# Another order of the instructions in the attention period, and another border to the FFN

## The chip, the cores and the metric

The kernel runs on one core of one Trainium2 chip. The metric is the device time of one execution in microseconds. TensorE (PE; its weight loads are PEld) multiplies and transposes, VectorE (DVE), ScalarE (ACT) and GpSimd (POOL) work on elements, SyncE (SP) issues the DMAs. Each engine works through its instructions in program order and waits on semaphores for the others.

## The reference

Attention with pooled queries, and a feed-forward network on its output.

```python
B, H, S, D = 4, 8, 1152, 64
q_pool = q.reshape(B, H, S // 2, 2, D).mean(axis=3)          # 576 queries per head
scores = 1 / sqrt(D) * q_pool @ k.T                          # 576 x 1152
scores = scores - scores.max(axis=-1)
attn = exp(scores); attn = attn / (attn.sum(axis=-1) + 1e-9)
x = (attn @ v) -> transposed to 2304 x 512
h = x @ w_in                                                 # 512 -> 2048
out = (h * tanh(softplus(h))) @ w_out                        # 2048 -> 512, float32
```

## The kernel before

**Attention.** The work is cut into 32 steps: batch (4), pair of heads (4), half of the queries (2). The two heads of a pair lie side by side in the partitions. A step has 9 chunks of 128 keys and 288 queries per head, and each chunk is one call of these functions:

- QK (L200): scores of a chunk, one matmul per head on 64 rows of the array each (shape 64*128), into a PSUM tile of the pool psS, which has two buffers; a chunk overwrites the tile of the chunk two before it.
- CP (L215) copies the scores to T3 in SBUF on ACT; MX (L218) keeps the running maximum over the chunks on DVE. Both read the PSUM tile.
- MT (L228), TMAX (L235), MB (L240): the maximum over the 128 keys of a chunk. Five transposes, one reduction on DVE, six transposes that spread the maximum over the partitions again (tile Mb in PSUM).
- SUB (L251, DVE) and EXP (L256, ACT): subtract and exponentiate, in four groups of 2, 2, 2 and 3 chunks (GR).
- PV (L270): values of a chunk, one matmul per head on 64 columns of the array each (shape 128*64), nine chunks added up in the PSUM tile pv, one buffer; PVE (L283, ACT) takes it out.
- ADD (L260, POOL) adds up the exponentials; FIN0 (L290) sums them over the partitions on TensorE, again in shape 128*64.
- FLN, FEX (ACT, logarithm and exponential), FU (POOL), FE, FX (DVE) multiply by the reciprocal of the sums and write xT. For the last step LX (L315) does it on DVE alone, with a reciprocal instruction.

Once per pair of steps QP (L122, POOL) pools the queries and TG (L139) transposes keys and queries, TGc (L153, ACT) takes them out. load_q, load_k and load_v issue the DMAs on SP.

**FFN.** x and the weights are split into a high and a low part (split_x, conv), H_ (L488) makes 12 matmuls of a hidden block, A_g, A_gh, D_gl the activation, O_ (L521) six matmuls of the output. 144 such blocks run after the attention; the first ones lie between the last values.

**What sets the order.** Every call is an entry of the list `plan` (L598 on) with a time in units of a step; the list is sorted by that time and called in that order. The times do nothing else: on the chip an engine takes its instructions in this order and as early as their semaphores allow. STEP (L337) has one time per call, added to the number of the step; PAIR (L397) the same per pair of steps. So parts of three steps overlap. XE (L569) places the first splits of x, TH and TA (L572) the first FFN blocks, LAST, LATE and GONE (L573 to L575) the end of the last two steps.

Of the kernel before, what the change touches and what calls it, by code (L numbers as in the profile page):

```python
# [12 lines left out]
ALU = mybir.AluOpType  # L13
# [4 lines left out]
def f32(ap):  # L18
    return ap.bitcast(F32)
# [3 lines left out]
def tile_pooled_attention_then_mish_ffn(ctx: ExitStack, tc: tile.TileContext, q, k, v, moe_w_in, moe_w_out, out):  # L23
# [5 lines left out]
    P = 128  # L29
# [37 lines left out]
    if True:  # L67
# [125 lines left out]
        rmaxs, Mbs, pvs, accs = {}, {}, {}, {}  # L193
# [46 lines left out]
        def MB(i):  # L240
            m = Ts.pop(i)
            Mb = ps1.tile([P, 2, 512], F32, tag="Mb", name=f"Mb{i}")
            for n, k0, k1, j, a in (
                (0, 0, P, 0, 0), (1, 0, P, 0, 128), (3, 0, P, 1, 64), (4, 0, P, 1, 160), (2, 0, 64, 0, 224), (2, 64, P, 1, 0)
            ):
                pe.transpose(  # L246
                    Mb[:, j, a:a + k1 - k0], m[k0:k1, n:n + 1].to_broadcast([k1 - k0, P]), ident[k0:k1, k0:k1]
                )
            Mbs[i] = Mb
# [20 lines left out]
        def PV(i, c):  # L270
            vn = vs[i // 2]
            if c == 0:
                pvs[i] = ps1.tile([P, 512], F32, tag="pv", name=f"pv{i}")
            for j in range(2):
# [4 lines left out]
                    start=(c == 0),  # L279
                    stop=(c == NC - 1),  # L280
# [48 lines left out]
        def FX(i):  # L329
# [8 lines left out]
            (QK, 0, -0.564),  # L338
            (CP, 0, -0.504),
            (QK, 1, -0.428),  # L340
            (MX, 1, -0.396),
            (CP, 1, -0.363),
            (QK, 2, -0.351),
            (MX, 2, -0.314),
            (QK, 3, -0.298),
            (CP, 2, -0.293),
            (MX, 3, -0.195),
            (QK, 4, -0.183),
            (CP, 3, -0.164),
            (CP, 4, -0.151),  # L350
            (MX, 4, -0.150),
            (QK, 5, -0.137),
            (CP, 5, -0.003),
            (QK, 6, 0.031),
            (MX, 5, 0.064),
            (CP, 6, 0.102),
            (QK, 7, 0.170),
            (MX, 6, 0.245),
            (CP, 7, 0.280),
            (MX, 7, 0.464),  # L360
            (QK, 8, 0.527),
            (CP, 8, 0.530),
            (MX, 8, 0.540),
            (MT, 0.653),
            (TMAX, 0.719),
            (MB, 0.814),
            (SUB, 1, 0.826),
            (SUB, 0, 0.867),
            (EXP, 1, 0.990),
            (SUB, 2, 1.091),  # L370
            (EXP, 0, 1.173),
            (PV, 0, 1.204),
            (PV, 1, 1.215),
            (ADD, 0, 1.267),
            (EXP, 2, 1.369),
            (SUB, 3, 1.494),
            (PV, 2, 1.536),
            (ADD, 1, 1.570),
            (PV, 3, 1.572),
            (EXP, 3, 1.607),  # L380
            (ADD, 2, 1.635),
            (PV, 4, 1.654),
            (PV, 5, 1.857),
            (PV, 6, 1.868),
            (ADD, 3, 1.906),
            (ADD, 4, 1.907),
            (PV, 7, 2.090),
            (FIN0, 2.105),
            (PV, 8, 2.130),
            (PVE, 2.178),  # L390
            (FLN, 2.247),
            (FEX, 2.397),
            (FU, 2.451),
            (FE, 2.604),
            (FX, 2.705),
        ]
        PAIR = [  # L397
            (QP, -2.081),
            (TG, 1, -1.246),
            (TGc, 1, -1.241),  # L400
            (TG, 2, -1.181),
            (TGc, 2, -1.088),
            (TG, 0, -1.039),
            (TGc, 0, -0.962),
            (TG, 3, -0.265),
            (TGc, 3, -0.240),
# [3 lines left out]
        ]  # L410

# [61 lines left out]
        def split_x(u, c):  # L473
# [5 lines left out]
            (dve if u > 2 and c in XD else pool).tensor_tensor(xl[:, c], src, f32(xh[:, c]), ALU.subtract)  # L479

# [84 lines left out]
        LW = -0.5  # L565
# [99 lines left out]
```

## Time and profile before

| | |
|---|---|
| runs, median (lowest to highest) | 896.43 us (896.0 to 898.17) |
| profiled execution: span from its first to its last instruction (the profile gives no other time of it) | 892.8 us |
| TensorE busy | 870.2 us, 97% of the span |
| VectorE busy | 596.7 us, 67% |
| ACT busy | 541.5 us, 61% |
| POOL busy | 455.8 us, 51% |
| mean granted TensorE clock | 0.993 |

The shares are means over two very different parts: in the attention, up to about 470 us, all four engines are busy; after it the FFN keeps TensorE busy alone. A TensorE instruction's end is modelled, its start is measured. "Idle before" is the time in which an engine had nothing to do before an instruction, with what ended it.

### The profile page before, as it was taken

How to read it: one execution, taken by the hardware profiler on the slowest of the kernel's cores; microseconds unless marked ns; L12 is line 12 of the kernel's file. 1: busy time of each engine (PE TensorE's matmuls, PEld its weight loads, DVE VectorE, ACT ScalarE, POOL GpSimd, SP SyncE). 2: the span in 40 equal slices, each digit the busy share in tenths (PEclk: the TensorE clock that was granted, in tenths of full speed). 3: DMA queues.
4: the chain of work that ended last, by engine and by line, in shares of the span. 5: the costliest groups of instructions: out<-in, count | busy, mean ns of one | idle time of the engine just before them, and what ended most of it. 6: DMA issues, size and time to landing. Idle time of an engine off the chain costs nothing. (4 is left out here: it accounts for less than half of the span.)

```text
span 892.8 us, 14677 instructions
## 1 busy us (share of the span) xinstructions
PE 870.2 (97%) x5668; PEld 589.5 (66%) x5668; DVE 596.7 (67%) x812; ACT 541.5 (61%) x999; POOL 455.8 (51%) x268
## 2 busy tenths in 40 slices
PE   6899999999999999999998999999999999999997
PEld 4444444444444444444446889999999999999996
DVE  4889988998889888998897753444455334432222
ACT  4788888888888888888888563333333233322221
POOL 1489888988889888998888530111111011100000
PEclk9899999999999999999999999999999999999999
DMA  6422323132321323131200120111112011001112
GB/s 177 130 49 59 80 54 80 27 81 54 80 59 49 80 54 80 28 80 54 75 2 1 48 94 9 57 48 32 55 65 71 24 48 48 24 1 48 48 48 70
DMA packets 75109, 50.74 MB, mean 57 GB/s; under 512 B 37408, under 2 KB 68640, under 8 KB 75040
## 3 DMA queue, kind: packets, MB, share of 16 engines
q1 hardware_dynamic: 75040, 49.82, 20.1%
q8 instruction: 44, 0.72, 0.3%
q14 instruction: 25, 0.20, 0.1%
HBM read 45.09 MB, written 4.72 MB: 56 GB/s over the span
## 5 line engine op out<-in xcount | busy, mean ns | idle before, releaser
L206 PE MATMUL s<-qT,kT 64*128 64x288 f32 x1152 | 210.7, 453 | 11.2 <-DVE rmax L223 7.2
L512 DVE TENSOR_TENSOR gl<-g,gh 128x256 fp32r<-128x256 f32 x144 | 68.8, 479 | 227.1 <-ACT gh L507 201.1
L502 ACT ACTIVATE g<-h 128x256 f32<-128x256 f32 x144 | 55.7, 387 | 242.5 <-PE h L497 242.5
L216 ACT COPY T<-s 128x576 f32<-128x576 f32 x288 | 181.2, 641 | 33.7 <-DVE rmax L223 15.2
L254 DVE TENSOR_TENSOR T<-T,Mb 128x1152 f32<-128x1152 f32 (+1 forms) x128 | 191.4, 1496 | 11.1 <-PE Mb L246 11.0
L275 PE MATMUL pv<-T,vn 128*64 128x288 f32 x1152 | 192.7, 425 | 1.9 <-ACT pvs L286 1.4
L223 DVE TENSOR_TENSOR rmax<-s,rmax 128x576 f32<-128x576 f32 x224 | 169.0, 754 | 34.2 <-ACT T L216 28.3
L460 POOL TENSOR_TENSOR wl<-wt,wh 128x512 fp32r<-128x512 f32 x32 | 41.8, 1308 | 251.8 <-ACT wh L457 207.9
L266 POOL TENSOR_TENSOR acc<-acc,T 128x1152 f32<-128x1152 f32 x64 | 168.9, 2638 | 2.7 <-ACT T L258 0.2
L258 ACT ACTIVATE T<-T 128x1152 f32<-128x1152 f32 (+1 forms) x128 | 165.9, 1296 | 6.8 <-DVE T L254 4.8
L206 PEld LDWEIGHTS s<-qT,kT 64*128 64x128 f32 x1152 | 89.3, 189 | 115.1 <-issue 40.4
L497 PE MATMUL h<-xh,wh 128*128 128x256 f32 x576 | 162.0, 281 | 0.0
L497 PE MATMUL h<-xh,wl 128*128 128x256 f32 x576 | 161.8, 281 | 0.0
L497 PE MATMUL h<-xl,wh 128*128 128x256 f32 x576 | 161.6, 281 | 0.0
L275 PEld LDWEIGHTS pv<-T,vn 128*64 128x64 f32 x1152 | 63.3, 135 | 88.4 <-issue 57.9
L497 PEld LDWEIGHTS h<-xh,wh 128*128 128x128 f32 x576 | 108.7, 189 | 8.1 <-issue 2.2
L497 PEld LDWEIGHTS h<-xl,wh 128*128 128x128 f32 x576 | 108.9, 189 | 6.0
L264 POOL TENSOR_TENSOR acc<-T 128x1152 f32<-128x1152 f32 x32 | 84.7, 2646 | 49.5 <-ACT T L258 46.0
L497 PEld LDWEIGHTS h<-xh,wl 128*128 128x128 f32 x576 | 109.2, 190 | 0.0
L530 PE MATMUL o<-wh,gh 128*128 128x512 f32 x146 | 57.8, 396 | 1.0 <-ACT xT L542 1.0
L530 PE MATMUL o<-wl,gh 128*128 128x512 f32 x146 | 57.5, 394 | 0.0
L530 PE MATMUL o<-wh,gl 128*128 128x512 f32 x146 | 57.3, 392 | 0.0
(381 smaller groups left out, 1101.2 us busy)
## 6 DMA issues: line engine op xcount, KB each, us to landing
qn<-in_q_dram SPq DMA_DIRECT2D x32, 288.0 KB, 3.8
vn<-in_v_dram SPq DMA_DIRECT2D x16, 576.0 KB, 4.9
kn<-in_k_dram SPq DMA_DIRECT2D x30, 288.0 KB, 4.1
ri<-in_moe_w_in_dram SPq DMA_DIRECT2D x64, 128.0 KB, 2.2
ro<-in_moe_w_out_dram SPq DMA_DIRECT2D x16, 512.0 KB, 3.5
out_dram<-xT SPq DMA_DIRECT2D x18, 256.0 KB, 2.6
T<-in_k_dram SPq DMA_DIRECT2D x2, 288.0 KB, 4.5
```

Source lines behind the costliest of these rows:

```text
L206: pe.matmul(s[:, j, 0:HQ], kT[64 * j:64 * j + 64, c], qT[64 * j:64 * j + 64, hf * HQ:(hf + 1) * HQ], start=True, stop=True,)
L216: act.copy(T3[:, i % 2, c], ss[i, c])
L223: dve.tensor_tensor(r, ss[i, c], T3[:, i % 2, 0] if c == 1 else r, ALU.max)
L254: dve.tensor_tensor(x, x, Mbs[i][:, :, 0:HQ].unsqueeze(1).to_broadcast([P, w, 2, HQ]), ALU.subtract)
L258: act.activation(x, x, AF.Exp, scale=0.0625)
L264: pool.tensor_tensor(accs[i], t[:, 0:2], t[:, 2:4], ALU.add)
L266: pool.tensor_tensor(accs[i], accs[i], t[:, 2 * n + 2:2 * n + 4], ALU.add)
L275: pe.matmul(pvs[i][64 * j:64 * j + 64, 0:HQ], vn[:, j, c, :], T3[:, i % 2, c, j], start=(c == 0), stop=(c == NC - 1),)
L497: pe.matmul(h[:, 0:UT], a, b, start=(m == 0), stop=(m == len(seq) - 1))
L502: act.activation(g, hs[bu, f], AF.Mish)
L512: dve.tensor_tensor(gl, ch.pop((bu, f)), f32(gs[bu, f][0]), ALU.subtract)
L530: pe.matmul(os_[bu][t], x, y, start=(first and m == 0), stop=(last and m == 2))
```

## The change

STEP gets two times per call, the first for even steps, the second for odd ones, so the two steps of a pair may have different orders. The times of STEP, PAIR and XE are new: score chunks mostly come in twos (6 and 7, 8 and the next step's 0, 1 and 2), value chunks in runs of two to four, and no longer from 0 to 8, so PV counts its calls to know the first and the last. MB gives its two 64-row transposes to a call of its own, MBb. split_x of the first three blocks becomes split_h (ACT) and split_l (POOL), 1.892 steps later. At the border the last two steps (BYREC) both end by FIN0 and LX; END gives times of their own to calls of steps 30 and 31; the first FFN blocks (TH, TA) and the reuse of memory (T_REST) move.

```diff
@@ -190,7 +190,7 @@
             load_q(1)
             load_k(1)
 
-        rmaxs, Mbs, pvs, accs = {}, {}, {}, {}
+        rmaxs, Mbs, pvs, pvn, accs = {}, {}, {}, {}, {}
 
@@ -240,12 +240,14 @@
         def MB(i):
             m = Ts.pop(i)
             Mb = ps1.tile([P, 2, 512], F32, tag="Mb", name=f"Mb{i}")
-            for n, k0, k1, j, a in (
-                (0, 0, P, 0, 0), (1, 0, P, 0, 128), (3, 0, P, 1, 64), (4, 0, P, 1, 160), (2, 0, 64, 0, 224), (2, 64, P, 1, 0)
-            ):
-                pe.transpose(
-                    Mb[:, j, a:a + k1 - k0], m[k0:k1, n:n + 1].to_broadcast([k1 - k0, P]), ident[k0:k1, k0:k1]
-                )
+            Mbs[i] = Mb, m
+            for n, j, a in ((0, 0, 0), (1, 0, 128), (3, 1, 64), (4, 1, 160)):
+                pe.transpose(Mb[:, j, a:a + P], m[:, n:n + 1].to_broadcast([P, P]), ident)
+
+        def MBb(i):
+            Mb, m = Mbs[i]
+            for k, j, a in ((0, 0, 224), (64, 1, 0)):
+                pe.transpose(Mb[:, j, a:a + 64], m[k:k + 64, 2:3].to_broadcast([64, P]), ident[k:k + 64, k:k + 64])
             Mbs[i] = Mb
 
         def SUB(i, g):
@@ -269,15 +271,16 @@
 
         def PV(i, c):
             vn = vs[i // 2]
-            if c == 0:
+            pvn[i] = pvn.get(i, 0) + 1
+            if pvn[i] == 1:
                 pvs[i] = ps1.tile([P, 512], F32, tag="pv", name=f"pv{i}")
             for j in range(2):
                 pe.matmul(
                     pvs[i][64 * j:64 * j + 64, 0:HQ],
                     vn[:, j, c, :],
                     T3[:, i % 2, c, j],
-                    start=(c == 0),
-                    stop=(c == NC - 1),
+                    start=(pvn[i] == 1),
+                    stop=(pvn[i] == NC),
                 )
 
@@ -335,79 +338,81 @@
 
         LQ, LK = -3.4, -2.2
         STEP = [
-            (QK, 0, -0.564),
-            (CP, 0, -0.504),
-            (QK, 1, -0.428),
-            (MX, 1, -0.396),
-            (CP, 1, -0.363),
-            (QK, 2, -0.351),
-            (MX, 2, -0.314),
-            (QK, 3, -0.298),
-            (CP, 2, -0.293),
-            (MX, 3, -0.195),
-            (QK, 4, -0.183),
-            (CP, 3, -0.164),
-            (CP, 4, -0.151),
-            (MX, 4, -0.150),
-            (QK, 5, -0.137),
-            (CP, 5, -0.003),
-            (QK, 6, 0.031),
-            (MX, 5, 0.064),
-            (CP, 6, 0.102),
-            (QK, 7, 0.170),
-            (MX, 6, 0.245),
-            (CP, 7, 0.280),
-            (MX, 7, 0.464),
-            (QK, 8, 0.527),
-            (CP, 8, 0.530),
-            (MX, 8, 0.540),
-            (MT, 0.653),
-            (TMAX, 0.719),
-            (MB, 0.814),
-            (SUB, 1, 0.826),
-            (SUB, 0, 0.867),
-            (EXP, 1, 0.990),
-            (SUB, 2, 1.091),
-            (EXP, 0, 1.173),
-            (PV, 0, 1.204),
-            (PV, 1, 1.215),
-            (ADD, 0, 1.267),
-            (EXP, 2, 1.369),
-            (SUB, 3, 1.494),
-            (PV, 2, 1.536),
-            (ADD, 1, 1.570),
-            (PV, 3, 1.572),
-            (EXP, 3, 1.607),
-            (ADD, 2, 1.635),
-            (PV, 4, 1.654),
-            (PV, 5, 1.857),
-            (PV, 6, 1.868),
-            (ADD, 3, 1.906),
-            (ADD, 4, 1.907),
-            (PV, 7, 2.090),
-            (FIN0, 2.105),
-            (PV, 8, 2.130),
-            (PVE, 2.178),
-            (FLN, 2.247),
-            (FEX, 2.397),
-            (FU, 2.451),
-            (FE, 2.604),
-            (FX, 2.705),
+            (QK, 0, -0.5640, -0.5584),
+            (CP, 0, -0.4042, -0.4268),
+            (QK, 1, -0.3837, -0.4118),
+            (QK, 2, -0.3395, -0.3676),
+            (MX, 1, -0.3197, -0.2976),
+            (MX, 2, -0.2628, -0.2408),
+            (CP, 1, -0.2498, -0.3491),
+            (CP, 2, -0.2033, -0.1585),
+            (QK, 3, -0.1849, -0.2352),
+            (QK, 4, -0.1407, -0.1056),
+            (MX, 3, -0.1181, -0.1833),
+            (MX, 4, -0.0612, -0.0387),
+            (CP, 3, -0.0587, -0.1195),
+            (QK, 5, 0.0172, -0.0614),
+            (CP, 4, 0.0823, 0.0864),
+            (MX, 5, 0.0835, 0.1060),
+            (CP, 5, 0.1429, 0.1655),
+            (QK, 6, 0.1527, 0.1835),
+            (QK, 7, 0.1969, 0.2277),
+            (MX, 6, 0.2282, 0.2507),
+            (MX, 7, 0.2850, 0.3076),
+            (CP, 6, 0.2876, 0.3102),
+            (CP, 7, 0.3445, 0.3722),
+            (QK, 8, 0.3974, 0.3918),
+            (MX, 8, 0.4747, 0.4973),
+            (CP, 8, 0.5342, 0.5567),
+            (MT, 0.5357, 0.5638),
+            (TMAX, 0.5963, 0.6255),
+            (MB, 0.6761, 0.7042),
+            (MBb, 0.7532, 0.7486),
+            (SUB, 0, 0.8666, 0.7871),
+            (EXP, 0, 0.9701, 0.9804),
+            (SUB, 1, 1.0113, 0.9887),
+            (SUB, 2, 1.1559, 1.1334),
+            (EXP, 1, 1.2264, 1.2039),
+            (PV, 0, 1.3117, 1.2407),
+            (ADD, 0, 1.3313, 1.3504),
+            (PV, 2, 1.3481, 1.4854),
+            (SUB, 3, 1.3575, 1.3349),
+            (EXP, 2, 1.4746, 1.4124),
+            (PV, 1, 1.4797, 1.3173),
+            (PV, 3, 1.5200, 1.3537),
+            (ADD, 1, 1.5913, 1.6104),
+            (EXP, 3, 1.6349, 1.6900),
+            (PV, 5, 1.7675, 2.1034),
+            (ADD, 2, 1.7928, 1.8231),
+            (PV, 8, 1.9331, 2.1397),
+            (PV, 4, 1.9734, 1.8085),
+            (ADD, 3, 1.9942, 2.0245),
+            (PV, 7, 2.0687, 2.0670),
+            (ADD, 4, 2.1024, 2.1328),
+            (PV, 6, 2.1090, 2.0267),
+            (PVE, 2.1820, 2.2046),
+            (FIN0, 2.2809, 2.2714),
+            (FLN, 2.3836, 2.4113),
+            (FEX, 2.4924, 2.4490),
+            (FE, 2.5303, 2.5472),
+            (FU, 2.5518, 2.5327),
+            (FX, 2.6512, 2.5981),
         ]
         PAIR = [
-            (QP, -2.081),
-            (TG, 1, -1.246),
-            (TGc, 1, -1.241),
-            (TG, 2, -1.181),
-            (TGc, 2, -1.088),
-            (TG, 0, -1.039),
-            (TGc, 0, -0.962),
-            (TG, 3, -0.265),
-            (TGc, 3, -0.240),
+            (QP, -1.7894),
+            (TG, 1, -1.2869),
+            (TGc, 1, -1.1948),
+            (TG, 2, -1.1438),
+            (TGc, 2, -1.0804),
+            (TG, 0, -1.0176),
+            (TGc, 0, -0.9498),
+            (TG, 3, -0.0969),
+            (TGc, 3, 0.0605),
             (load_q, LQ),
             (load_k, LK),
             (load_v, 0.2),
         ]
+
 
         pieces = [(f, io) for io in range(2) for f in range(BLK[0])]
         pieces += [(f, io) for f in range(BLK[0], NF) for io in range(2)]
@@ -478,6 +483,13 @@
             act.copy(xh[:, c], src)
             (dve if u > 2 and c in XD else pool).tensor_tensor(xl[:, c], src, f32(xh[:, c]), ALU.subtract)
 
+        def split_h(u, c):
+            act.copy(x_tiles(u)[0][:, c], xT[:, c, u * UT:(u + 1) * UT])
+
+        def split_l(u, c):
+            xh, xl = x_tiles(u)
+            pool.tensor_tensor(xl[:, c], xT[:, c, u * UT:(u + 1) * UT], f32(xh[:, c]), ALU.subtract)
+
         def acc(n):
             u, t = divmod(n, UT // P)
             w = DM // UT
@@ -562,17 +574,35 @@
 
         CV2 = [0, 0, 0, 1, 2, 3]
         CV3 = [0, 1, 2, 3, 4, 5]
-        LW = -0.5
+        LW, REUSE = -0.5, -0.438
         XD, ED = (2, 3), ()
         CVD = [4, 6, 6, 8, 9, 10]
         SPL = [0, 0, 1, 1]
-        XE = [10.955 + 2 * n for n in range(9)] + [28.955, 29.955, 30.6]
+        XE = [5.349, 7.349, 9.349, 11.349, 13.349, 15.349, 17.349, 19.349, 21.349, 23.349, 25.349, 27.349]
+        XL = 1.892
         XT = (-0.20, -0.19, -0.18, -0.17)
-        T3F, DT, XS, T_REST = 1.14, 0.2, 0.5, 1.76
-        TH, TA = (-0.30, -0.05, 0.60), 0.62
-        LAST = {FIN0: 1.70, LX: 1.75}
-        LATE = {FIN0: 0.60, FLN: 0.62, FEX: 0.63, FU: 0.65, FE: 0.66, FX: 0.70}
-        GONE = (FIN0, FLN, FEX, FE, FU, FX)
+        T3F, DT, XS, T_REST = 1.14, 0.2, 0.5, 1.92
+        TH, TA = (-0.31, 0.22, 0.47), 0.52
+        BYREC = (NS - 2, NS - 1,)
+        GONE = [(i, fn) for i in BYREC for fn in (FLN, FEX, FE, FU, FX)]
+        END = {
+            (PV, NS - 1, 0): 0.25,
+            (PV, NS - 1, 1): 0.26,
+            (PV, NS - 1, 2): 0.33,
+            (PV, NS - 1, 3): 0.34,
+            (PV, NS - 1, 4): 0.5,
+            (PV, NS - 1, 5): 0.51,
+            (PV, NS - 1, 6): 0.7,
+            (PV, NS - 1, 7): 0.71,
+            (PV, NS - 1, 8): 0.72,
+            (EXP, NS - 1, 3): 0.45,
+            (PVE, NS - 2): 0.21,
+            (EXP, NS - 1, 1): 0.2,
+            (FIN0, NS - 2): 0.6,
+            (LX, NS - 2): 0.62,
+            (FIN0, NS - 1): 1.87,
+            (LX, NS - 1): 1.9,
+        }
         FLOW = [
             (H_, 0), (convs, 0), (A_g, 0), (A_gh, 0), (D_gl, 0), (split,), (O_, 3), (EV, 3, 0), (convs, 1),
             (convs, 5), (convs, 4), (convs, 3), (convs, 2), (EV, 3, 1),
@@ -596,11 +626,14 @@
             open_pool("x3", 1)
 
         plan = []
-        for fn, *a, t in STEP:
-            plan += [(i + t, fn, i, *a) for i in range(NS - 1 if fn not in LATE else NS - 2)]
-            plan += [(NS - 1 + t, fn, NS - 1, *a)] if fn not in GONE else []
-        plan += [(NS + t, fn, NS - 1) for fn, t in LAST.items()]
-        plan += [(NS + t, fn, NS - 2) for fn, t in LATE.items()]
+        for fn, *a, t0, t1 in STEP:
+            t = t0, t1
+            for i in range(NS):
+                if (i, fn) in GONE:
+                    continue
+                plan.append((i + t[i % 2], fn, i, *a))
+        plan += [(0, LX, i) for i in BYREC]
+        plan = [((NS + END[fn, *a] if (fn, *a) in END else t), fn, *a) for t, fn, *a in plan]
         for fn, *a, t in PAIR:
             first_p = 2 if fn in (load_q, load_k) else 0 if fn is load_v else 1
             plan += [(2 * p + t, fn, p, *a) for p in range(first_p, B * NP)]
@@ -613,9 +646,10 @@
         for n, t in enumerate(CONV0):
             plan += [(t[m], conv, n, m) for m in range(6)]
         plan += [(NS + LW, load_w, n) for n in (4, 5)]
-        plan += [(t, split_x, n // 4, n % 4) for n, t in enumerate(XE)]
+        plan += [(t, split_h, n // 4, n % 4) for n, t in enumerate(XE)]
+        plan += [(t + XL, split_l, n // 4, n % 4) for n, t in enumerate(XE)]
         plan += [(NS + XT[c], split_x, 3, c) for c in range(NKC)]
-        plan += [(NS - 0.44, reuse_qk), (NS - 0.44, reuse_psS), (NS + T_REST, reuse_rest)]
+        plan += [(NS + REUSE, reuse_qk), (NS + REUSE, reuse_psS), (NS + T_REST, reuse_rest)]
         for g in range(len(seq) + 8):
             t = NS + T3F + DT * (g - 3)
             for fn, *a in FLOW:
```

## Rows read from the trace of the kernel before

**Rows 1.** Busy time by stage: stretch, each engine's busy us, granted clock, DMA
```profile
15.00:30.00 15.00, 8.59 (x33) 3.84 (x33) 11.93 (x20) 8.01 (x14) 3.81 (x3) 0.68 0.50 149
85.00:435.00 350.00, 348.59 (x2319) 164.61 (x2316) 315.46 (x369) 299.59 (x464) 309.42 (x170) 1.00 0.24 60
```

**Rows 2.** Timeline of TensorE's matmuls in mid attention: start, duration, what
```profile
258.52 0.66 PE L146 MATMUL xt<-identr,kn 128*128 128x128 f32 x4
259.01 0.80 PE L246 MATMUL Mb<-identr,m 128*128 128x128 f32 x6
259.65 0.71 PE L206 MATMUL s<-qT,kT 64*128 64x288 f32 x4
...
262.12 0.71 PE L275 MATMUL pv<-T,vn 128*64 128x288 f32 x4
262.75 0.66 PE L146 MATMUL xt<-identr,kn 128*128 128x128 f32 x4
...
264.03 0.71 PE L275 MATMUL pv<-T,vn 128*64 128x288 f32 x4
264.56 0.66 PE L297 MATMUL Sb<-acc,cst 128*64 128x288 f32 x4
265.05 0.66 PE L275 MATMUL pv<-T,vn 128*64 128x288 f32 x4
265.63 0.76 PE L206 MATMUL s<-qT,kT 64*128 64x288 f32 x4
266.32 1.19 PE L275 MATMUL pv<-T,vn 128*64 128x288 f32 x8
267.44 1.28 PE L206 MATMUL s<-qT,kT 64*128 64x288 f32 x8
268.65 0.71 PE L275 MATMUL pv<-T,vn 128*64 128x288 f32 x4
269.42 0.76 PE L206 MATMUL s<-qT,kT 64*128 64x288 f32 x4
```

**Rows 3.** Timeline of VectorE: the maximum of step 1 and of step 30
```profile
43.82 0.82 DVE L237 TENSOR_REDUCE m<-mt 128x5 f32<-128x640 f32 x1
...
457.94 0.81 DVE L237 TENSOR_REDUCE m<-mt 128x5 f32<-128x640 f32 x1
```

**Rows 4.** Groups of instructions: busy us, mean ns, idle before and releaser
```profile
L223 DVE TENSOR_TENSOR rmax<-s,rmax 128x576 f32<-128x576 f32 x224 | 169.0, 754 | 34.2 <-ACT T L216 28.3 <-PE s L206 0.7
...
L258 ACT ACTIVATE T<-T 128x1728 f32<-128x1728 f32 x32 | 52.7, 1647 | 0.9 <-DVE T L254 0.8
...
L157 ACT COPY kT<-xt 128x512 f32<-128x512 f32 x30 | 17.6, 587 | 17.4 <-PE xt L146 17.4
```

**Rows 5.** Timeline: a score chunk on TensorE and the copy waiting for it
```profile
462.09 0.76 PE L206 MATMUL s<-qT,kT 64*128 64x288 f32 x4
...
462.95 0.64 ACT L216 COPY T<-s 128x576 f32<-128x576 f32 x1 [0.17 <-PE s L206]
```

**Rows 6.** Timeline of TensorE and its weight loads at the border: three idle gaps
```profile
469.56 0.77 PE L232 MATMUL mt<-identr,rmax 128*128 128x128 f32 x5 [1.14 <-DVE rmax L223]
...
478.48 2.16 PE L275 MATMUL pv<-T,vn 128*64 128x288 f32 x16 [1.40 <-ACT pvs L286]
...
522.42 0.19 PEld L530 LDWEIGHTS o<-wh,gh 128*128 128x128 f32 x1 [1.16 <-ACT xT L542]
```

**Rows 7.** Timeline of VectorE and POOL at the border
```profile
484.19 6.55 DVE L512 TENSOR_TENSOR gl<-g,gh 128x256 fp32r<-128x256 f32 x3 [4.13 <-ACT gh L507]
...
504.86 1.95 DVE L320 RECIPROCAL rs<-rs 128x288 f32<-128x288 f32 x1
...
484.03 5.47 POOL L266 TENSOR_TENSOR acc<-acc,T 128x1152 f32<-128x1152 f32 x2
```

**Rows 8.** Waits by pair: us in total, times, longest us
```profile
PEld s L206 <- DVE rmax L223: 36.9, 80, 2.8
```

## The prediction

> **What bounds the kernel now.** I read the page first, then the table by stage, then TensorE's instructions over one pair of steps, then the idle gaps at the two borders of the attention part. In the middle of attention all four engines look busy: of 350 us TensorE 348.6, VectorE 315.5, POOL 309.4, ACT 299.6 [rows 1]. The page warns that matmul ends are modelled, so the 99.6% alone prove nothing; the starts do. Over a pair of steps TensorE's blocks start one behind the other, and each gap between starts comes back whenever the same two kinds of block follow one another [rows 2]. I take a block's price from its own start to the next block's start:
>
> - a score chunk (QK) alone: 0.69 (265.63 to 266.32); two in a row: 1.21 (267.44 to 268.65), not 1.38. A join saves 0.16.
> - a value chunk (PV) alone: 0.63 (262.12 to 262.75); two in a row: 1.12 (266.32 to 267.44), not 1.26. A join saves 0.14; with the row sums (FIN0, same tile shape) in between the three take 0.53 + 0.49 + 0.58 = 1.60 (264.03 to 265.63), 0.29 less than three alone.
> - the block of four transposes 0.49 when another 128x128 block follows, the six of MB 0.64.
>
> Such prices with no other wait add up to the period, which the reductions of the row maxima give: 43.82 to 457.94 is 29 steps, so 28.56 us for a pair of steps [rows 3]. The one misfit is the 0.77 of the value chunk at 268.65 before the next score (0.14 over its price, once per step). So TensorE, in program order, sets the period, and it pays for changes of tile shape: 64-row scores, 64-column values, full transposes. VectorE needs 315.46 x 28.56/350 = 25.74 us per pair, POOL 25.25, ACT 24.45 [rows 1]: a shorter TensorE period has 2.8 us of room before VectorE.
>
> The Trainium skill, TensorEngine Tiling (Array Packing), Key Properties, says that a change of tiling mode drains the array. It gives no price; the 0.14 to 0.16 of a join are this trace's.
>
> **Period, part by part.** The work is unchanged: 18 score chunks, 18 value chunks, the transposes, the sums. I sort both tables and count the blocks per pair of steps.
>
> Scores: before, 14 stand alone and 2 pairs exist (8 of one step with 0 of the next). After: pairs 6-7 and 8-0 and 1-2 in both steps, 4-5 in even, 3-4 in odd steps: 8 pairs, 2 alone. 6 more joins x 0.16 = 0.96; one single that goes stood behind MB at 0.64, not 0.69: I take 0.90.
>
> Values: before, 10 alone, twice 0-1, twice 7-FIN0-8. After: even 7-6, 0-FIN0-1-3, 2, 4, 6-7-5-8; odd FIN0-0-2, 1-3, 5, 8-4. Joins between value or FIN0 blocks: 2 + 4 = 6 before, 7 + 4 = 11 after; 5 more x 0.15 (0.14 in a pair, 0.29 / 2 in three) = 0.75.
>
> Transposes: MBb cut off from MB costs nothing in even steps (TG1 takes the place beside MB, the next score block goes on in MBb's 64-row shape); in odd steps a value chunk follows it, one more change of shape. TG3 loses its place beside MB, one more. Neither order stands in the trace; a change costs 0.14 to 0.16 where it does, nothing if it hides behind the weight load. I take 0.10 each: -0.20.
>
> Net 0.90 + 0.75 - 0.20 = 1.45 us per pair; TensorE's period becomes 27.11. If the two late value chunks (0.14 each) go as well, it is 26.83 (1.73).
>
> **What else could be late at 27.11.** A score is ready for its readers 0.86 after it starts (462.09 to 462.95) [rows 5], and a score buffer is free when CP (0.64) and MX (0.75) have read it [rows 4, 5]. MT behind QK 8: TensorE gives 1.21 + 0.63 = 1.84, MX 8 needs 0.86 + 0.75 = 1.61: in time. The tightest place is QK 4 of even steps, which needs CP 2: on ACT stand CP 1 (ready 0.86 after QK 1), EXP 3 (1.65), TGc1 (0.59), CP 2 [rows 4]. That is 0.86 + 0.64 + 1.65 + 0.59 + 0.64 = 4.38 without overlap; TensorE gets there after 1.21 + 0.49 + 0.64 + 0.64 + 0.63 + 0.49 = 4.10. So between no wait (ACT's instructions overlap a little) and 0.28 per pair. I take none. PVE, waited for before the first value chunk, gets two score chunks as cover in place of one (1.21 against 0.69). POOL's order is nearly the old one; QP moves 0.29 of a step later, still 0.65 of a step ahead of its transposes and 0.39 ahead of the next load_q, which overwrites its source, so SP's queue isn't held. The x split, once per pair, takes the same ACT and POOL time; three of twelve leave the last steps for the middle.
>
> 15 pairs (14.5 by the maxima, and step 31, whose scores still run) x 1.45 = 21.8 us. Bounds: 15 x 1.73 = 26.0; with the wait at QK 4, 15 x 1.17 = 17.6.
>
> **Border to the FFN.** TensorE stands three times: 1.14 at MT(31) for the last maximum, 1.40 at PV(31,0) for PVE(30), 1.16 at 522.42 for an ACT copy [rows 6]. H_(0,1) moves directly ahead of PV(31,0); such a block lasts longer than the 1.40, so this goes. MT's wait keeps its cause, the third hangs on the weight conversions, which keep their order. Step 30 now ends like step 31: FLN, FEX (with two ACT table loads around it), FU, FE and FX go, LX(30) comes: its reciprocal alone is 1.95 on VectorE [rows 7], and gl and the conversions queue behind it. FFN blocks feed TensorE ahead of need there, so I charge 0.4 and take -1.0; bounds -3.7 (all three go) and, next, the lock.
>
> Row first: three gl subtractions of 0.48 each took 6.55 at 484.19, beside two POOL adds from 484.03 to 489.50 [rows 7]. The Trainium skill, SBUF — State Buffer, section SBUF: two separate sides, has the rule: VectorE and POOL share a port pair under an exclusive lock, and a VectorE instruction with two SBUF inputs waits out a POOL one. The trace agrees with the rule. Without it LX(30) costs its own time, with it its last instruction (two SBUF inputs) and the gl behind it wait for an add of step 31 each, 5.5 for two adds: that is rival 3.
>
> **Fill.** From 15 to 30 us neither engine is full: TensorE 8.59, VectorE 11.93 of 15 [rows 1], and the granted clock averages 0.68, so part of it runs at 1.2 GHz, after the first waits of the scores. In the new order conv 0 comes ahead of MX 3, and the maximum of step 0 ahead of two maxima of step 1. At best VectorE's 3.1 idle go, at worst as much comes; I take -0.5.
>
> **Sum.** -21.8 - 1.0 - 0.5 = -23.3: span 892.8 to 869.5. The profile gives the profiled execution's span alone; the median of the runs lies 3.6 above it (896.43 - 892.8), which I keep: 873.1, said as 873. A difference of 0.3% (2.7 us) is about what can be told from no change.
>
> **Rivals.**
> 1. *VectorE becomes the bound.* The idle before the maxima, 34.2 us or 2.14 per pair [rows 4], is put down to ACT's copies; if all of it stays, the pair takes 25.74 + 2.14 = 27.88, the gain is 0.68 x 15 = 10.2 + 1.5, the time 884.7. For: at 27.11 VectorE is 95% full and scores come in bursts. Against: the maxima now stand in pairs as well.
> 2. *The score ring turns against the change (slower).* A joined second chunk starts earlier by the value chunk that stood between (0.63), while its buffer's readers need not. The trace has 80 waits of scores for maxima, 36.9 us [rows 8]. If each of the 6 new pairs waits 0.63, that is 3.78 per pair of steps, 15 x 3.78 = 56.7 more than forecast: 930. It decides from (1.45 + 0.10)/6 = 0.26 per new pair on. Against: the walk above finds one place, not six.
> 3. *The lock at the border*: VectorE's queue late by two adds and TensorE behind it, 873 + 5.5 = 878.5. For: the 6.55 us. Against: FU leaves POOL and two table loads leave ACT there.
> 4. *The change does not do what it says*: a join saves only the modelled wait and TensorE's array is paced by the columns alone; then 896. Against: starts, not ends, give 1.21 and 1.12.
> 5. *More*: 26.0 + 3.7 + 3.1 = 32.8 us: 863.6.
>
> **How the numbers follow.** Forecast 0.62 (868 to 879 by itself), rival 1 0.17, rival 2 0.04, rival 3 0.08, rival 4 0.03, rival 5 0.06. Faster 0.62 + 0.17 + 0.08 + 0.06 = 0.93, same 0.03, slower 0.04. The range 866 to 885 leaves out rivals 2 and 4, half of rival 1's spread and half of rival 5: under 0.2.
>
> **What would show it.** Right: maxima two steps apart by 27.0 to 27.3 us; score pairs at 1.21 and value runs at 1.12 and 2.1; VectorE above 94% in the middle; no wait at PV(31,0). Wrong: a period of 27.7 or more with TensorE waiting for rmax or T (rivals 1, 2); VectorE's LX or gl lasting over 2 us and TensorE idle after 480 us (rival 3). The prediction falls if joined blocks keep their gaps, or if TensorE's waits per pair exceed 0.7 us.

## The result, and the profile after

The changed kernel takes 880.51 us (median; 879.31 to 881.09) against 896.68 for the kernel before on the same chip: ratio 0.9821, interval 0.9805 to 0.9837, a gain of 16.2 us. The forecast was 873, with a range of 866 to 885. The profiled execution has a span of 878.9, which is 13.9 less than before; 23.3 less was forecast. Each span is that of a single execution: before's lies 3.6 under the median that the forecast started from, after's 1.6 under its own. So the forecast is missed by 7.4 us in the medians and by 9.4 us in the spans.

To see where the 9.4 us are, I cut the span at four marks that both traces have: the copy of a finished value tile (ACT, pvs<-pv) of steps 1 and 29, the first output block of the FFN, and the end.

| stretch | before, us | after, us | difference | forecast |
|---|---|---|---|---|
| start to values of step 1 (fill) | 65.95 | 66.83 | +0.9 | -0.5 |
| to values of step 29 (14 pairs of steps) | 398.91 | 381.26 | -17.7 | 14 x -1.45 = -20.3 |
| to the first output block (one more pair, border) | 21.92 | 24.34 | +2.4 | -1.45 - 1.0 |
| to the end | 405.98 | 406.45 | +0.5 | 0 |

So the middle did nearly what was forecast, and the border has the wrong sign. The +0.9 of the fill is one execution against one: four kernels below differ from after only at the border, and in their traces the same fill ends at 65.57, 65.90, 67.09 and 67.27, so its sign is open. The middle's -17.7 is 1.26 per pair, a little less than the steady difference below, because the last of before's 14 pairs was short (27.40).

Busy time by stage of the changed kernel, columns as in [rows 1]:

```profile
15.00:30.00 15.00, 8.29 (x32) 3.88 (x30) 11.53 (x17) 8.31 (x14) 5.57 (x4) 0.62 0.48 150
85.00:435.00 350.00, 350.00 (x2431) 180.62 (x2431) 331.62 (x387) 313.07 (x488) 324.95 (x180) 1.00 0.25 65
```

VectorE rose from 90% to 94.7% of the middle. The maximum of step 1 and of step 30 in the timeline of VectorE, against [rows 3]:

```profile
44.77 0.83 DVE L237 TENSOR_REDUCE m<-mt 128x5 f32<-128x640 f32 x1 [1.69 <-PE mt L232]
...
439.73 0.83 DVE L237 TENSOR_REDUCE m<-mt 128x5 f32<-128x640 f32 x1 [0.43 <-PE mt L232]
```

29 steps now take 394.96 us, 27.24 per pair of steps where 28.56 was; 27.11 was forecast. The blocks of TensorE behind it (timeline of its matmuls over a part of a pair, to be read by starts as in [rows 2]):

```profile
219.19 1.24 PE L206 MATMUL s<-qT,kT 64*128 64x288 f32 x8
220.36 0.71 PE L278 MATMUL pv<-T,vn 128*64 128x288 f32 x4
221.06 0.77 PE L232 MATMUL mt<-identr,rmax 128*128 128x128 f32 x5
221.79 1.30 PE L206 MATMUL s<-qT,kT 64*128 64x288 f32 x8
223.02 0.65 PE L245 MATMUL Mb<-identr,m 128*128 128x128 f32 x4
...
227.75 2.16 PE L278 MATMUL pv<-T,vn 128*64 128x288 f32 x16
229.84 1.30 PE L206 MATMUL s<-qT,kT 64*128 64x288 f32 x8
231.07 0.70 PE L300 MATMUL Sb<-acc,cst 128*64 128x288 f32 x4
...
242.94 1.47 PE L206 MATMUL s<-qT,kT 64*128 64x288 f32 x8
244.33 0.71 PE L278 MATMUL pv<-T,vn 128*64 128x288 f32 x4
```

A pair of scores without a wait takes 1.17 (219.19 to 220.36), less than the 1.21 of before; but most pairs take 1.23 to 1.26 (221.79, 229.84) and one 1.39 (242.94). Four value chunks in a row take 2.09. What the scores wait for is in the waits by pair:

```profile
PEld s L206 <- ACT T L216: 74.7, 205, 2.2
ACT T L216 <- DVE rmax L223: 46.1, 91, 2.7
```

The 80 waits of scores for maxima of [rows 8] have gone but for one of 0.3; scores wait for the copies (CP), and the copies for the maxima (MX). The new list also turns the two readers of a score tile round, which the description of the change doesn't say: by the timelines of ACT and VectorE, the maximum ran ahead of the copy on 96 of the 256 tiles that both read before, and on 240 after. The waits between the two, before:

```profile
DVE rmax L223 <- ACT T L216: 29.1, 58, 1.8
ACT T L216 <- DVE rmax L223: 15.2, 33, 1.7
```

After, the first of these is down to 3.9, and the second is the 46.1 above.

### The profile page after: what moved, and what is told of

It reads as the page before. It is cut to its first block, busy times and chain, and to the rows that moved or that the text cites. A ratio compares the mean times of both kernels' runs of the same rounds, so it can differ in the third digit from the quotient of the medians.

```text
span 878.9 us, 14807 instructions
## 1 busy us (share of the span) xinstructions
PE 856.1 (97%) x5668; PEld 601.2 (68%) x5668; DVE 601.9 (68%) x813; ACT 536.2 (61%) x995; POOL 455.2 (52%) x267
## 5 line engine op out<-in xcount | busy, mean ns | idle before, releaser
L524 DVE TENSOR_TENSOR gl<-g,gh 128x256 fp32r<-128x256 f32 x144 | 65.3, 453 | 225.3 <-ACT gh L519 199.0
L216 ACT COPY T<-s 128x576 f32<-128x576 f32 x288 | 180.9, 641 | 52.2 <-DVE rmax L223 46.1
L206 PE MATMUL s<-qT,kT 64*128 64x288 f32 x1152 | 195.8, 449 | 8.4 <-ACT T L216 7.2
L278 PE MATMUL pv<-T,vn 128*64 128x288 f32 x1152 | 175.0, 422 | 2.5 <-ACT pvs L289 2.5
L278 PEld LDWEIGHTS pv<-T,vn 128*64 128x64 f32 x1152 | 72.4, 137 | 71.4 <-issue 28.0
```

The source lines that it names most:

```text
L206: pe.matmul(s[:, j, 0:HQ], kT[64 * j:64 * j + 64, c], qT[64 * j:64 * j + 64, hf * HQ:(hf + 1) * HQ], start=True, stop=True,)
L216: act.copy(T3[:, i % 2, c], ss[i, c])
L278: pe.matmul(pvs[i][64 * j:64 * j + 64, 0:HQ], vn[:, j, c, :], T3[:, i % 2, c, j], start=(pvn[i] == 1), stop=(pvn[i] == NC),)
L524: dve.tensor_tensor(gl, ch.pop((bu, f)), f32(gs[bu, f][0]), ALU.subtract)
```

## The experiments

For the steady part I use one measure throughout: the time from each matmul's start to the next one's, summed by kind over ten pairs of steps and divided by ten. Waits and changes of shape are in it, so the kinds add up to the period. (Before's ten pairs hold one of 28.87; the others take 28.56.) The runs were spread over several chips, on which before took 895.41 to 896.68, and the fill alone differs by 1.7 from one execution to another; so a difference of 1 or 2 us between two kernels is read from this table and from the stretches, not from the times.

| us per pair of steps | scores | values, row sums | MT | MB, TG | period |
|---|---|---|---|---|---|
| before | 11.93 | 12.10 | 1.39 | 3.17 | 28.59 |
| after | 11.25 | 11.14 | 1.45 | 3.39 | 27.23 |
| e1_split (joins taken back) | 12.19 | 11.51 | 1.39 | 3.39 | 28.48 |
| e6_mbb (MBb behind MB) | 11.20 | 11.14 | 1.45 | 3.64 | 27.43 |
| e11_odd (one order) | 13.46 | 11.12 | 1.39 | 4.23 | 30.19 |
| e5_halfmax (half maxima) | 10.73 | 11.06 | 1.39 | 3.39 | 26.58 |
| e12_load (load alone) | 11.56 | 11.12 | 1.39 | 3.39 | 27.47 |

**Joins taken back.** Some score pairs and value runs are cut again by moving values between them.

```diff
-            (PV, 0, 1.3117, 1.2407),
+            (PV, 0, 1.3117, 1.1900),
-            (PV, 2, 1.3481, 1.4854),
+            (PV, 2, 1.3481, 1.4200),
-            (PV, 1, 1.4797, 1.3173),
+            (PV, 1, 1.4100, 1.3173),
-            (FIN0, 2.2809, 2.2714),
+            (FIN0, 2.2809, 2.2056),
```

> Against the changed kernel, only TensorE's order differs: in both steps of a pair the score pairs 6-7 and 8-0 are split by a value (or row-sum) block that is taken from the run next to them. Four joined scores and three joined values less per pair of steps. Theory 1 (TensorE's changes of shape set the period): 4 x 0.15 + 3 x 0.15 = 1.05 us more per pair, the period goes from 27.23 to 28.28, the time up by 15 x 1.05 = 15.8, to about 896. Theory 2 (VectorE, or the reading of the score buffers, sets the period and TensorE has slack): the period stays within 0.2 of 27.23, the time within 3 us of 880.5.

Measured 898.36 (896.66 to 899.58), ratio to before 1.0025 (1.0014 to 1.0036), period 28.48. Four moved times, with all work the same, give back the whole gain: 0.94 in the scores and 0.37 in values and row sums. That the order of neighbours on TensorE is worth the gain is shown by this. Not all of it is change of shape: 0.26 of the 0.94 is a wait of a value chunk for ACT's copy of the value tile, once per pair of steps, that the edit brought with it.

**MBb directly behind MB**, so that the transposes stay together and MBb loses the place in front of a score.

```diff
-            (MBb, 0.7532, 0.7486),
+            (MBb, 0.6762, 0.7043),
```

> MBb goes back directly behind MB in every step, as in the old order; all else is the changed kernel's. Theory 1 (each change of tile shape costs 0.1 to 0.15): in even steps TG1 then stands behind the 64-row transposes and score 3 behind TG1, one change more, 0.15 per pair, in odd steps nothing: 15 x 0.15 = 2 us slower. Theory 2 (the place of MBb matters for when VectorE can subtract): in odd steps nothing changes, in even steps SUB 0 could start earlier but waits for the maximum of chunk 3 anyway: no difference over 0.5 us.

Measured 883.43 (882.59 to 884.88), ratio 0.9870 (0.9854 to 0.9886): 2.9 us more than after. The transposes take 0.25 more per pair, the scores 0.05 less; 0.20 x 14.5 = 2.9. In the new order cutting MBb off is worth 0.20 per pair, where I had charged it 0.10.

**One order for both steps of a pair**: the times of odd steps in both columns.

> Both steps of a pair get the odd steps' times. By the blocks' prices, against the changed kernel: one joined score pair less (+0.15), one joined value more (-0.15), the 64-row transposes beside a score in both steps (-0.1): 27.1. Theory 1 (the prices alone decide; keeping odd and even steps apart is worth nothing by itself): a period of 27.1 to 27.3, within 3 us of 880.5. Theory 2 (the two steps need different orders since only even steps have the key transposes and their copies on ACT): waits of TensorE appear, the period is 27.6 or more, 5 us or more slower.

Measured 926.27 (925.53 to 928.03), ratio 1.0350 (1.0334 to 1.0365): 30 us slower than before. TensorE's idle gaps in the timeline of its matmuls, over one pair of steps:

```profile
216.31 0.76 PE L206 MATMUL s<-qT,kT 64*128 64x288 f32 x4 [0.57 <-ACT T L216]
221.36 0.71 PE L278 MATMUL pv<-T,vn 128*64 128x288 f32 x4 [0.45 <-ACT pvs L289]
227.49 0.65 PE L245 MATMUL Mb<-identr,m 128*128 128x128 f32 x4 [0.29 <-DVE m L237]
231.70 0.76 PE L206 MATMUL s<-qT,kT 64*128 64x288 f32 x4 [0.78 <-ACT T L216]
236.16 0.71 PE L278 MATMUL pv<-T,vn 128*64 128x288 f32 x4 [0.45 <-ACT pvs L289]
242.28 0.65 PE L245 MATMUL Mb<-identr,m 128*128 128x128 f32 x4 [0.28 <-DVE m L237]
```

They sum to 2.82 of the 2.96 by which the period exceeds that of after. The scores' 1.35 is rival 2's mechanism, scores waiting for their tiles; 0.90 is late value copies and 0.57 late maxima. This fits that the joins pay only where each step's copies are placed around the work that its step has. The times of the list PAIR stayed, so the transposes of keys fall between other blocks than in either column; the run doesn't separate that from the order of the step itself.

**Half of the maxima's work**: from chunk 2 on MX takes half of the columns, so the maximum is over a part of the scores.

```diff
-            dve.tensor_tensor(r, ss[i, c], T3[:, i % 2, 0] if c == 1 else r, ALU.max)
+            h = HQ if c < 2 else HQ // 2
+            dve.tensor_tensor(r[:, :, 0:h], ss[i, c][:, :, 0:h], (T3[:, i % 2, 0] if c == 1 else r)[:, :, 0:h], ALU.max)
```

> The maxima of chunks 2 to 8 run over half of the columns only (part of the maximum is left out), so VectorE has some 14 x 0.3 = 4.2 us less per pair of steps and a score buffer is free 0.3 us sooner. Theory 1 (TensorE's blocks set the period, waits add 0.2 to 0.3): the period falls from 27.23 to the sum of the unwaited block prices, 26.9 to 27.0, the time by 3.5 to 5 us from 880.5. Theory 2 (VectorE or the score buffers set it): the period falls by more than 0.6, below 26.6, and the time by 9 us or more.

Measured 866.79 (866.41 to 867.33), ratio 0.9683 (0.9668 to 0.9697), 13.7 us below after. The period is 26.58, 0.65 less, which makes 9.4 over 14.5 pairs; nearly all of it (0.52) is in the scores, and every pair of scores takes 1.17. The values of step 1 end at 62.05, 4.8 us earlier. So in the changed kernel VectorE's part of the chain holds TensorE by 0.65 us per pair. Two causes fit: VectorE as such is late, or a score tile is read for too long, because its two readers come one after the other. The timeline of after shows the second in a pair of scores:

```profile
229.84 1.30 PE L206 MATMUL s<-qT,kT 64*128 64x288 f32 x8
...
230.78 1.61 DVE L223 TENSOR_TENSOR rmax<-s,rmax 128x576 f32<-128x576 f32 x2
231.62 0.64 ACT L216 COPY T<-s 128x576 f32<-128x576 f32 x1
232.46 0.64 ACT L216 COPY T<-s 128x576 f32<-128x576 f32 x1
```

The first copy starts 1.78 after the scores, when the first maximum (0.75) has ended, and not at 0.86 as the copy of [rows 5].

**The load alone**: half maxima as above, and VectorE gets time back by a reduction that touches no score tile.

```diff
+            if c in (2, 4, 7):
+                d = p1.tile([P, 2], F32, tag="d", name=f"d{i}_{c}")
+                dve.tensor_reduce(d, r[:, :, 0:240], axis=AX.X, op=ALU.max)
```

> As in the kernel with half maxima (the maxima of chunks 2 to 8 take half of the columns, 0.37 us instead of 0.75, 866.8 us), but VectorE gets the time back elsewhere: behind the maxima of chunks 2, 4 and 7 it reduces 480 columns of the running maximum in SBUF, an instruction that reads no score tile and whose result nobody uses. VectorE's load returns to about that of the changed kernel (94%), the score tiles are still read for half as long. Theory 'readers' (the 0.65 us per pair of steps that half maxima gave came from tiles that become free earlier): the period stays at 26.6 to 26.8, the time is 867 to 870. Theory 'load' (VectorE as such was late, rival 1): the period returns to 27.2, the time to 878 to 881.

Measured 883.16 (881.43 to 884.13), ratio 0.9852 (0.9835 to 0.9869). The period is 27.47, even above after's 27.23. Busy time of the middle, half maxima first, then with the load (columns as in [rows 1]):

```profile
85.00:435.00 350.00, 349.29 (x2483) 191.32 (x2481) 290.67 (x398) 315.77 (x499) 331.03 (x183) 1.00 0.25 65
```

```profile
85.00:435.00 350.00, 347.25 (x2412) 181.04 (x2408) 324.49 (x461) 306.36 (x483) 322.83 (x178) 1.00 0.25 65
```

VectorE goes from 83% to 92.7% and the gain is gone, though each tile is read for as short a time as with half maxima. So shorter reads alone don't keep the gain; it matters when VectorE comes to its maxima. Its busy share alone doesn't tell: 92.7% here goes with a longer period than 94.7% in after. The path to TensorE is the same: in the middle the copies wait 35.1 us for maxima, against 30.6 in after and 18.0 with half maxima. The added reductions stand at three fixed places of a step, and at other places they might cost less. Not tested is the other remedy, the copies ahead of the maxima, as on 160 tiles of before.

**Border: values of step 30 taken out earlier** (PVE of step 30 ahead of EXP 1 of step 31).

```diff
-            (PVE, NS - 2): 0.21,
+            (PVE, NS - 2): 0.19,
```

> One number of the border differs: PVE(30) stands ahead of EXP 1 of step 31 on ACT, not behind it. Theory 1 (TensorE's 2.51 us of idling ahead of the first value chunk of step 31 hang on ACT's order): PVE then runs right after EXP 0, the first two value chunks start behind the second FFN block, some 1.2 us of idling remain before chunk 2, and if TensorE's clock no longer drops there another 1.5 us go: 1.3 to 2.8 us faster than 880.5. Theory 2 (the border hangs on VectorE's chain to the last exponentials and the FFN activations behind them): the idling moves behind, the first output block starts as before, no difference over 0.5 us.

Measured 879.31 (878.65 to 881.37), ratio 0.9818 (0.9805 to 0.9832), which can't be told from after. The border stretch shrinks from 24.34 to 21.53, and the next one grows from 406.45 to 408.53: TensorE stands later for sums (0.58) and for gl (1.48) instead.

**Border: the late split off VectorE's queue.** The two subtractions xl of the fourth block that VectorE does go behind SUB 3 of step 31.

```diff
-            pool.tensor_tensor(xl[:, c], xT[:, c, u * UT:(u + 1) * UT], f32(xh[:, c]), ALU.subtract)
+            (dve if u > 2 else pool).tensor_tensor(xl[:, c], xT[:, c, u * UT:(u + 1) * UT], f32(xh[:, c]), ALU.subtract)
...
-        plan += [(NS + XT[c], split_x, 3, c) for c in range(NKC)]
+        plan += [(NS + XT[c], split_h if c in XD else split_x, 3, c) for c in range(NKC)]
+        plan += [(NS + 0.46, split_l, 3, c) for c in XD]
```

> The two x subtractions on VectorE at the border (the low parts of block 3) move from between SUB 0 and SUB 1 of step 31 to behind SUB 3, where VectorE idles 3.7 us in the changed kernel. Theory 1 (these two, 2.59 us long, are what makes EXP 1, then PVE and the first value chunk of step 31 late): SUB 1 starts 2.5 us earlier, the idling of 2.51 us on TensorE goes, with it the drop of the clock: 2.5 to 4 us faster than 880.5. Theory 2 (TensorE waits for ACT's order alone): at most 0.5 us faster.

Measured 876.79 (876.39 to 878.79), ratio 0.9785 (0.9771 to 0.9798): 3.7 us below after by the medians, and the fastest kernel here that leaves nothing out. The border stretch is 20.33, 4.0 less; TensorE no longer stands at PV(31,0). The next stretch gives 1.5 back (407.95), so 2.5 is gained by the stretches, and the rest lies within the scatter. Its rows, VectorE first, then the TensorE block that waits:

```profile
465.68 6.09 DVE L524 TENSOR_TENSOR gl<-g,gh 128x256 fp32r<-128x256 f32 x3 [1.83 <-ACT gh L519]
...
466.00 2.65 POOL L266 TENSOR_TENSOR acc<-T 128x1152 f32<-128x1152 f32 x1 [2.77 <-ACT g L514]
...
478.97 0.50 PE L542 MATMUL o1x<-wh,gl 128*128 128x512 f32 x1 [1.15 <-DVE gl L524]
```

**Both border edits at once.**

> Both border edits at once: PVE of step 30 ahead of EXP 1 of step 31 (alone 879.3) and the late splits of block 3 on VectorE (alone 876.8). Theory 'one wait': both edits remove the same 2.51 us wait of the values of step 31, so together they give no more than the better one, 876 to 878. Theory 'two causes': they add, 874 to 875.5.

Measured 878.00 (877.29 to 878.42), ratio 0.9798 (0.9782 to 0.9814). The border stretch is 20.24, against 20.33 with the late split alone: they remove the same wait and don't add.

**The late split, and the row sums of step 30 earlier** (FIN0 at 0.49 for 0.60, to let POOL's adds of step 31 begin earlier).

> On top of e3_xlate, FIN0(30), the row sums of step 30, goes ahead of the value chunks 4 and 5 of step 31. The one buffer of the row sums' additions is free after it, so POOL's adds of step 31 start 1.1 us earlier. Theory 1 (VectorE's work at the border is stretched by the port it shares with POOL's adds, and TensorE's idling of 1.15 us behind gl at 479 in e3_xlate comes from that): the adds end 1.1 us earlier, the conversions on VectorE with them, 0.5 to 1.2 us faster than e3_xlate (876.8). Theory 2 (the idling hangs on VectorE's own work, above all the reciprocal of step 30): no difference over 0.4 us from e3_xlate.

Measured 877.85 (877.17 to 878.53), ratio 0.9806 (0.9791 to 0.9821): no gain over the late split alone. The three gl subtractions take 7.93 there, against 6.09: the adds came earlier and met them in full.

**Fill: all of step 0 in the old order.**

> Step 0 gets the times of the old order, all other steps keep the new ones. Theory 1 (the first step's new order costs the 0.9 us by which step 1 ends later than before, since its copies stand behind maxima and these behind weight conversions): step 1 ends 0.9 us earlier or more, the time falls by 0.9 to 2 us from 880.5. Theory 2 (the loss comes from step 1's own order): no difference over 0.5 us.

Measured 887.93 (885.83 to 888.35), ratio 0.9906 (0.9892 to 0.9920); the values of step 1 end at 74.04, 7.2 later. What makes it so much later was not taken apart; the run says nothing on the cause of the 0.9 us.

**Fill: only the scores and maxima of step 0 in the old order.**

> Step 0 takes the old times for its scores, copies, maxima and transposes alone (QK, CP, MX, MT, TMAX, MB); everything else, the values of step 0 too, keeps the new times. In the changed kernel the values of step 1 end 0.9 us later than before. Theory 'order of step 0': the fill of before comes back, end of the values of step 1 at 65.9 in place of 66.8, the time 879.6. Theory 'clock' (TensorE's gaps of 0.34, 1.46 and 0.30 us between the scores of step 1 lower the granted clock at 38 to 44 us, whatever step 0 does): the end stays at 66.8 or later, the time is 880.5 or more.

Measured 880.20 (879.95 to 880.98), ratio 0.9823 (0.9808 to 0.9837); the values of step 1 end at 66.69, as in after (66.83). TensorE's gaps of 1.40 and 0.30 and a granted clock of 0.72 from 38 to 44 us stay, so the order of step 0 isn't what makes these. On the 0.9 us itself the run can't decide, since the fill of after ends anywhere between 65.57 and 67.27 in the traces that have it.

## Why the prediction was right, and where not

**The middle: right, by two errors that nearly cancel.** The forecast was -1.45 per pair of steps; -1.36 came by the table above (-1.32 by the maxima, 28.56 to 27.24). Block by block:

- *Joins were worth more than I took.* Without waits the order takes 26.58 (half maxima), 2.0 under before. I took 0.16 per score join from 1.21 [rows 2], but that pair held a short wait; free of it, it is 2 x 0.69 - 1.17 = 0.21. Scores would have gained 1.20 (11.93 to 10.73), not 0.90. Values and row sums gained 0.96, not 0.75; the late value chunk of [rows 2] (0.77) went with them, which I had kept for the range.
- *The transposes* cost 0.22 more, 0.20 were taken, but not from the parts that I named: MBb, charged 0.10, saves 0.25 on them (e6_mbb), and the other new places cost the more.
- *VectorE takes 0.65 back.* This is the mechanism of rival 1, at 0.65 where its 27.88 stood for 0.77, and it hid because the joins gave as much more. I had written that VectorE has 2.8 us of room. The rival's own measure, the 34.2 us of idle before the maxima [rows 4], did fall, and VectorE is late all the same. It fell as the maxima now mostly stand first: what VectorE waited for copies, the copies now wait for it. At 94.7% it isn't full and yet late, since its work is wanted in bursts. The row of their group (columns as in [rows 4]):

```profile
L223 DVE TENSOR_TENSOR rmax<-s,rmax 128x576 f32<-128x576 f32 x224 | 168.9, 754 | 10.9 <-PE s L206 0.9
```

The step that failed in form, though not in its sum, is the walk over the score tiles: it let CP and MX start together 0.86 after their scores. They run one after the other, on every tile of both traces, so a tile is held longer than the walk said, and VectorE's lateness reaches TensorE through ACT's copy. That is why scores wait for ACT in the waits by pair, and why the tightest place was not QK 4 of even steps alone. That the walk came out near is luck of two sizes. Rival 1 is true as a mechanism at nearly its own price, hidden by the joins. Rival 2 is real as a mechanism (the kernel with one order) but not in this order; rival 4 falls with the joins taken back.

**The border: wrong, +2.4 where -2.45 was forecast.** I removed the 1.40 at PV(31,0) [rows 6] because a longer block was put in front. But what PV(31,0) waits for, PVE(30), moved back too. TensorE's gaps at the border, then the chain behind the second, from the timeline of POOL, VectorE and ACT:

```profile
452.85 0.76 PE L232 MATMUL mt<-identr,rmax 128*128 128x128 f32 x5 [0.43 <-DVE rmax L223]
...
462.62 3.67 PE L278 MATMUL pv<-T,vn 128*64 128x288 f32 x16 [2.51 <-ACT pvs L289]
...
508.53 0.19 PEld L542 LDWEIGHTS o<-wh,gh 128*128 128x128 f32 x1 [1.18 <-ACT xT L554]
```

```profile
453.25 5.39 POOL L268 TENSOR_TENSOR acc<-acc,T 128x1152 f32<-128x1152 f32 x2
...
457.22 2.59 DVE L484 TENSOR_TENSOR xl<-xT,xh 128x256 fp32r<-128x256 f32 x2
459.73 4.47 DVE L256 TENSOR_TENSOR T<-T,Mb 128x1152 f32<-128x1152 f32 x3
...
461.11 1.16 ACT L260 ACTIVATE T<-T 128x1152 f32<-128x1152 f32 x1 [2.61 <-DVE T L256]
462.18 0.39 ACT L289 ACTIVATE pvs<-pv 128x288 f32<-128x288 f32 x1
```

The wait at MT(31) shrank from 1.14 to 0.43, and the third stayed, as forecast. In ACT's order PVE(30) stands behind EXP 1 of step 31, which waits 2.61 for its SUB; that SUB stands behind two late splits xl, 2.59 us long beside POOL's adds. To read it: the releaser of the gap (pvs) had not been slow itself, its predecessor had waited, and so on back to the queue where nothing waits any more. The granted clock fell after this gap (0.58 from 462 to 464, 0.57 from 464 to 466, toward the lower level of 1.2 GHz), while it was 1.00 there in the kernel with the late split; the sixteen value matmuls took 3.67 instead of 2.16. 2.51 + 1.51 = 4.0, just what that kernel gained in this stretch; the stretch came 4.85 above its forecast, and the other 0.85 was not taken apart. The granted clock is the third number from the end (columns as in [rows 1]), after first, then with the late split:

```profile
462.00:464.00 2.00, 1.38 (x6) 0.77 (x8) 2.00 (x2) 1.62 (x3) 1.25 (x1) 0.58 0.00 0
464.00:466.00 2.00, 2.00 (x12) 0.94 (x8) 0.20 (x1) 1.69 (x2) 0.00 (x0) 0.57 0.00 0
```

```profile
462.00:464.00 2.00, 2.00 (x18) 1.56 (x14) 1.84 (x2) 1.95 (x2) 1.23 (x1) 1.00 0.00 0
```

So the failed step is "this goes": I looked at what stood in front of PV(31,0) on TensorE, and not at the queue in front of its releaser on ACT.

The lock (rival 3) is in the trace, but not where I put it. LX(30) was hardly hindered, and three gl subtractions took 1.53 with the idle time between them (0.43 each, where I had written 0.48), where [rows 7] had 6.55, since POOL's adds of step 31 came after them; the weight conversions met the adds in their place (VectorE and POOL):

```profile
467.94 1.53 DVE L524 TENSOR_TENSOR gl<-g,gh 128x256 fp32r<-128x256 f32 x3 [3.74 <-ACT gh L519]
...
470.05 1.95 DVE L323 RECIPROCAL rs<-rs 128x288 f32<-128x288 f32 x1
...
475.54 3.06 DVE L449 SCALAR_TENSOR_TENSOR wt<-ri,wt 128x512 int32<-128x512 int32 x1
...
472.43 5.62 POOL L268 TENSOR_TENSOR acc<-acc,T 128x1152 f32<-128x1152 f32 x2
```

The adds are that late because FIN0(30) reads the one buffer of acc that they overwrite: it ends at 469.51, and the first add starts at 469.70. Nothing waited long for the conversions (+0.5 to the end). In the kernel with the late split the adds are back beside gl, 6.09, and TensorE stands 1.15: the price of rival 3 is about a fifth of its 5.5. The Trainium skill, SBUF — State Buffer, section SBUF: two separate sides, tells of the lock that VectorE and POOL share; 1.53 without and 6.09 beside the adds agree with it.

**The fill: +0.9 for -0.5, but its sign is open.** In after's trace the maximum of step 0 came 1.4 earlier (27.85 for 29.21). Then the scores of step 1 wait for copies, and the blocks behind run long (TensorE's timeline of after):

```profile
37.17 0.76 PE L206 MATMUL s<-qT,kT 64*128 64x288 f32 x4 [1.46 <-ACT T L216]
38.23 0.76 PE L206 MATMUL s<-qT,kT 64*128 64x288 f32 x4 [0.30 <-ACT T L216]
38.91 2.10 PE L278 MATMUL pv<-T,vn 128*64 128x288 f32 x8
40.94 1.97 PE L206 MATMUL s<-qT,kT 64*128 64x288 f32 x8
42.84 1.19 PE L278 MATMUL pv<-T,vn 128*64 128x288 f32 x8
```

Two values take 2.03 and two scores 1.90, 1.6 more together than at the upper level (1.12 and 1.17); the granted clock of 38 to 44 us averages 0.72, where before had 1.00. Without these 1.6 this execution's fill would be at -0.8. I had weighed the clock only up to 30 us. But the kernel with the earlier PVE, which has the same fill, shows the same gaps (0.30, 1.46 and 0.30) and nearly the same clock, and its fill ends at 65.90, where before's single trace has 65.95. It was ahead already when the score chunk of 34.37 started, at 33.50. The stretch in after, then in that kernel:

```profile
38.00:44.00 6.00, 5.77 (x29) 2.71 (x29) 4.81 (x5) 4.46 (x7) 4.49 (x2) 0.72 0.67 173
```

```profile
38.00:44.00 6.00, 6.00 (x33) 2.94 (x33) 4.09 (x5) 4.36 (x7) 5.28 (x2) 0.74 0.44 128
```

So the clock costs 1.6 here, and whether the fill as a whole gained or lost isn't shown: over the five traces it lies between -0.4 and +1.3 of before's one. What lowers the clock isn't settled: half maxima have a gap of 1.22 in the same place and keep 1.00.

**From the span to the time.** The forecast kept the 3.6 us between before's span and its median; after's are 1.6 apart. This term, which has nothing to do with the change, brought the time 2.0 nearer to the forecast than the spans are: luck.

## What to carry to other kernels

Price a reordering by start-to-start sums per kind of block, before and after: they add up to the period, and they separate what joins save from what waits take back. When an engine gets faster, walk the chain of the next one with its readers one behind the other. At a border, follow the releaser of a gap back through its own queue before calling the gap gone: the wait here was made by two small subtractions on VectorE, two queues away from TensorE. And before explaining a microsecond at the start of a kernel, look at the same stretch in several executions: here it differed by 1.7 with nothing changed.

## What was not expected of the hardware

- Two engines that read the same score tile in PSUM ran one after the other in this program: MX at 230.78, its CP at 231.62, with waits of CP for MX of 46.1 us in all. On none of the 256 tiles of either trace do the two overlap. It is the program that orders them: before, each of the 96 copies that stood behind their maximum waits for a semaphore that VectorE's maximum sets. What the chip would do without it no run here tells.
- A gap of 2.51 us on TensorE cost 1.5 us more behind it, by a granted clock of 0.57 to 0.58 over the next 4 us. Before, a gap of 1.40 in front of the same value chunks left it at 1.00.
